# Moving the last batch's transposes to SyncE's queue, with a new instruction order, in a kernel for gated linear attention followed by a mixer

## The chip, the cores and the metric

One Trainium2 chip, one of its cores. The metric is device time in microseconds (us). A run more than 1.5% above the fastest of its kernel counts as slow and is left out of the ratios (the medians given are of all runs). The kernel before took 174.36 us (median of 3 runs, 174.34 to 175.11); its profiled execution took 174.75 us, of which the profile's span covers 173.0 us.

## The reference

```python
state = alpha[:, :, t, :, None] * state + einsum('bhd,bhe->bhde', k[:, :, t], v[:, :, t])   # for t in 768 steps
y[:, :, t] = einsum('bhd,bhde->bhe', q[:, :, t], state)
# x = y with heads side by side: (4 batches, 768, 384)
h = x.transpose(0, 2, 1) @ U @ V              # low rank (32), along the sequence
u = x + h.transpose(0, 2, 1)
out = u + maximum(u @ w_ch1, 0) @ w_ch2       # 384 -> 1536 -> 384
```

Four batches, 8 heads of 48, 768 steps. The kernel works in chunks of 128 steps, six to a batch.

## The kernel before

The program does not fix the order of its instructions by hand. Each step is added to a plan with a cost for each engine that may run it, a priority, what it reads and what it writes. A list scheduler then picks, at each moment of its own model of time, the step that can start first, and emits the instructions in that order. Semaphores are added afterwards, so a wrong cost in the plan gives no wrong result; it gives a wait on the chip.

```python
if eng == "SP":                                  # a DMA issued by SyncE
    dma = max(dma, t + 600.0) + cost
    clock[eng] = max(t + 450.0, dma - 3500.0)
    end = dma + 2000.0
...
if eng == "PE" and "PE" in u.engs:
    u.est = max(u.est, end)
else:
    u.est = max(u.est, done + u.slack)           # slack: 150 ns for batches 1 to 3
```

For one chunk of the recurrence (q and k are scaled by the decays, transposed, multiplied into scores):

```python
P.add({"PE": mm(*[C] * 4)}, lambda e: f_tr(rk, tk), r=[rk], w=[tk], ...)      # 4 transposes into PSUM
P.add({"PE": mm(*[C] * 4)}, lambda e: f_tr(rq, tq), r=[rq], w=[tq], ...)
P.add({"DVE": 335, "ACT": 500}, lambda e: f_ev(e, kT, tk), r=[tk], w=[kT], ...)  # eviction to SBUF
P.add({"DVE": 335, "ACT": 500}, lambda e: f_ev(e, qT, tq), r=[tq], w=[qT], ...)
...
P.add({"PE": mm(*[C] * 4)}, f_sc, r=[kT, qT], w=[sc[0], sc[1]], mode="R", ...)   # the score block
```

The mixer of a batch: `utx` is the low-rank sum over all chunks of x; each chunk gets a low-rank matmul and the addition that makes u; u is transposed on TensorE into uT; 72 matmuls of 384 columns (u with w_ch1) and 72 more (with w_ch2) follow. The multiplications of one batch are scheduled among the recurrence of the next, and `LEAD` says how far behind the recurrence their priority is:

```python
LEAD = 3.0
def mlp_prio(b, x):
    return ((b + 1) * NC + LEAD + x * NC) * 100.0
```

## Time and profile before

| | before |
|---|---|
| median time | 174.36 us |
| span of the profile | 173.0 us |
| first matmul of a multiplication (with w_ch1, first batch) | 30.69 us |
| end of the last matmul | 169.49 us |
| the stretch between these two | 138.80 us |
| TensorE idle within it | 2.86 us |

The prediction shows most of what matters. These three stretches add where the idle time lies. In such a line come the stretch, its length, and busy us (with the number of instructions) of PE, PEld (weight loads), DVE, ACT and POOL, then the granted clock, the DMA share and GB/s. Length less PE busy is idle: 2.23, 0.63 and 0 us.

```profile
31.00:60.00 29.00, 26.77 (x373) 16.97 (x374) 24.44 (x54) 21.73 (x57) 13.08 (x21) 1.00 1.03 259
60.00:100.00 40.00, 39.37 (x490) 26.72 (x488) 28.24 (x55) 27.73 (x68) 18.76 (x25) 1.00 1.11 203
100.00:140.00 40.00, 40.00 (x414) 25.89 (x413) 26.75 (x50) 21.82 (x52) 10.91 (x13) 1.00 0.36 85
```

### The profile page before, as it was taken

The page shows a single profiled execution, that of the slowest core. Times are in us where ns is not written, and L with a number is a line of the kernel's source. Part 1 is how long each engine was busy: PE and PEld are TensorE (multiplying, and loading weights), DVE is VectorE, ACT ScalarE, POOL GpSimd, SP SyncE. Part 2 cuts the span into 40 slices and gives each one's busy share as a digit, 9 for nine tenths or more (in the row PEclk, how much of TensorE's full clock was granted, in tenths as well). Part 3 has the DMA queues.
Part 4 walks back from the last instruction along what each step waited for, and adds up shares of the span by engine and source line. Part 5 has one row for each costly group of instructions (what it writes and reads, how often), then busy time and mean ns, then how long its engine had stood idle before and what let it go on. Part 6 is the DMA issues. An engine that isn't in the chain of part 4 may idle for free.

```text
span 173.0 us, 4823 instructions
## 1 busy us (share of the span) xinstructions
PE 161.9 (94%) x1862; PEld 104.2 (60%) x1862; DVE 109.0 (63%) x232; ACT 104.1 (60%) x247; POOL 59.5 (34%) x97
## 2 busy tenths in 40 slices
PE   7688998899996999999998999999999999999991
PEld 2355765566564776676676657666666566656560
DVE  4589685598996986958675559976474294000231
ACT  4588773779785767558949436638783210996000
POOL 8056366247331765255155414910430000000000
PEclk9999699999999999999999999999999999999998
DMA  5999989999998999999989999611000212100222
GB/s 140 266 249 260 267 255 335 258 300 330 269 267 200 178 207 211 214 222 221 230 147 206 189 166 258 170 58 37 0 0 4 91 45 91 51 0 0 91 93 91
DMA packets 83031, 28.82 MB, mean 167 GB/s; under 512 B 76832, under 2 KB 82976, under 8 KB 83008
## 3 DMA queue, kind: packets, MB, share of 16 engines
q1 hardware_dynamic: 83008, 28.52, 72.0%
q8 instruction: 14, 0.23, 0.6%
q14 instruction: 9, 0.07, 0.2%
HBM read 23.79 MB, written 4.72 MB: 165 GB/s over the span
## 4 chain that ended last, share of the span: by engine, by line
PE 60%; DMA 19%; SPq 15%; issue 2%; POOL 1%; ACT 1%; DVE 0%; ACTq 0%; POOLq 0%
PE ps L772 27%; PE ps L749 16%; SPq L342 10%; DMA io<-in_v_dram 8%; DMA io<-in_moe_w_ch_dram 5%; SPq L317 3%; DMA io<-in_alpha_dram 3%; PE ps L584 3%; DMA io<-in_k_dram 3%; PE ps L605 2%; PE ps L712 2%; PE ps L722 2%; PE ps L664 1%; PE ps L554 1%; PE ps L418 1%
## 5 line engine op out<-in xcount | busy, mean ns | idle before, releaser
L749 PE MATMUL ps<-uT,w_sb 128*128 128x384 bf16 x288 | 53.1, 326 | 0.0
L772 PE MATMUL ps<-w_sb,h1t 128*128 128x384 bf16 x288 | 52.8, 326 | 0.0
L759 ACT ACTIVATE h1t<-ps 128x384 bf16<-128x384 f32 x73 | 35.2, 494 | 8.8 <-PE ps L749 8.5
L772 PEld LDWEIGHTS <-h1t 128*128 128x128 bf16 x288 | 26.1, 98 | 16.0 <-issue 1.0
L749 PEld LDWEIGHTS <-w_sb 128*128 128x128 bf16 x288 | 26.1, 98 | 15.4
L779 DVE TENSOR_TENSOR ou<-ub,ps 128x384 f32<-128x384 bf16 x24 | 13.2, 551 | 27.6 <-PE ps L772 27.3
L302 POOL CAST rv<-io 128x384 bf16<-128x384 f32 x19 | 11.2, 590 | 35.7 <-DMA io<-in_v_dram 30.7
L615 DVE TENSOR_TENSOR pm<-ps,maskc 128x512 bf16<-128x512 f32 x24 | 15.7, 685 | 6.7 <-PE ps L605 6.5
L572 POOL TENSOR_TENSOR rk<-io,ai 128x384 bf16<-128x384 f32 x12 | 11.0, 916 | 20.2 <-ACT ai L565 18.7
L761 DVE TENSOR_SCALAR h1t<-ps 128x384 bf16<-128x384 f32 x23 | 12.6, 552 | 7.4 <-PE ps L749 4.8
L456 DVE TENSOR_TENSOR pm<-ps,maskp 128x512 bf16<-128x512 f32 x24 | 15.8, 681 | 0.7 <-ACT h1t L759 0.5
L298 ACT CAST xb<-ps 128x192 bf16<-128x192 f32 (+1 forms) x23 | 8.8, 392 | 11.6 <-PE ps L664 7.6
L298 ACT COPY kt<-ps 128x512 bf16<-128x512 bf16 x17 | 10.0, 586 | 5.8 <-PE ps L584 5.3
L713 DVE TENSOR_TENSOR ub<-xb,ps 128x384 bf16<-128x384 bf16 x24 | 12.1, 547 | 1.2 <-PE ps L712 1.2
L298 ACT COPY qt<-ps 128x512 bf16<-128x512 bf16 x17 | 11.3, 663 | 1.6 <-PE ps L418 1.0
L302 POOL CAST w_sb<-io 128x384 bf16<-128x384 f32 x21 | 10.8, 527 | 3.8 <-DMA io<-in_moe_w_ch_dram 3.5
L572 POOL TENSOR_TENSOR rq<-io,aa 128x384 bf16<-128x384 f32 x12 | 11.6, 967 | 0.0
L375 ACT ACTIVATE lt<-io 128x384 bf16<-128x384 f32 x12 | 6.4, 530 | 5.2 <-DMA io<-in_alpha_dram 5.2
L298 ACT COPY uT<-ps 128x768 bf16<-128x768 bf16 x4 | 3.2, 799 | 8.6 <-PE ps L722 5.1
L547 ACT ACTIVATE lt<-io 128x384 bf16<-128x384 f32 x12 | 6.5, 542 | 2.0 <-DMA io<-in_alpha_dram 2.0
L398 ACT ACTIVATE ai<-ps 128x384 bf16<-128x384 f32 x12 | 5.9, 493 | 2.8 <-PE ps L391 2.8
L565 ACT ACTIVATE ai<-ps 128x384 bf16<-128x384 f32 x12 | 6.0, 500 | 2.4 <-PE ps L557 2.0
(114 smaller groups left out, 249.3 us busy)
## 6 DMA issues: line engine op xcount, KB each, us to landing
io<-in_alpha_dram SPq DMA_DIRECT2D x24, 192.0 KB, 4.3
io<-in_k_dram SPq DMA_DIRECT2D x24, 192.0 KB, 4.5
io<-in_q_dram SPq DMA_DIRECT2D x24, 192.0 KB, 4.3
io<-in_v_dram SPq DMA_DIRECT2D x24, 192.0 KB, 4.5
io<-in_moe_w_ch_dram SPq DMA_DIRECT2D x24, 192.0 KB, 4.4
out_dram<-ou SPq DMA_DIRECT2D x24, 192.0 KB, 1.9
u_in<-in_moe_U_dram SPq DMA_DIRECT2D x1, 96.0 KB, 4.6
v_in<-in_moe_V_dram SPq DMA_DIRECT2D x1, 96.0 KB, 4.3
```

The lines of the kernel that those rows point to most:

```text
L298: nc.scalar.copy(dst, src)
L302: nc.gpsimd.tensor_copy(dst, src)
L342: lambda e: nc.sync.dma_start(t().rearrange("p (h j) d -> p h (j d)", j=2), src[b, hs, sl, :].rearrange("h (p j) d -> p h (j d)", j=2)),
L456: nc.vector.tensor_tensor(dst, s2, maskp.to_broadcast([C, 2, 2, C]), op=ALU.mult)
L572: eng.tensor_tensor(dst()[:, :, 0:D], a(), x(), op=ALU.mult)
L615: nc.vector.tensor_tensor(pm()[:, :, par, :], s2, maskc.to_broadcast([C, HP, C]), op=ALU.mult)
L713: P.add({"DVE": 465}, lambda e, c=c, hb=hb: nc.vector.tensor_tensor(ub()[:, c, :], xb()[:, c, :], hb()[:, 0:DM], op=ALU.add), r=[hb] + xk( ...
L749: nc.tensor.matmul(hb()[:, 0:TW], lhsT=w1_sb[:, ct, jt * 128 : (jt + 1) * 128], rhs=uT()[:, ct, tt * TW : (tt + 1) * TW], start=(ct == 0), ...
L759: nc.scalar.activation(dst, hb()[:, 0:TW], AF.Relu)
L761: nc.vector.tensor_scalar_max(dst, hb()[:, 0:TW], 0.0)
L772: nc.tensor.matmul(hb()[:, 0:DM], lhsT=h1()[:, jt, c * C : (c + 1) * C], rhs=w2_sb[:, jt, :], start=(jt == 0), stop=(jt == NJ - 1),)
L779: P.add({"DVE": 468}, lambda e: nc.vector.tensor_tensor(ou(), ub()[:, c, :], hb()[:, 0:DM], op=ALU.add), r=[hb, (ub, c)], w=[ou], prio=-100)
```

## The change

Its intent: take transposes off TensorE in the last batch, as the loads run out, by letting DMAs issued by SyncE transpose from SBUF to SBUF (through what is called the crossbar here); make the plan's order sturdier (slack, a bonus for staying in the matmul mode, buffers taken to be free 200 ns later) and its cost for loads higher; and add the first batch's low-rank sums within the output's PSUM group instead of in VectorE.

```diff
+    EASE = 200.0
+    STAY = 20.0                         # TensorE: prefer the mode it is in
+    TRD = {(3, c) for c in range(2, NC)}   # q, k of these chunks by crossbar
+    SL = 300.0                          # slack, 150 before
+    TRU = (3,)                          # u of this batch by crossbar
+            if eng == "SP" and op.mode == "X":
+                dma = max(dma, t) + cost
+                clock[eng] = t + cost
+                end = dma + 850.0
-                b.last = max(b.last, done)
+                b.last = max(b.last, done + self.EASE)
-    LEAD = 3.0
+    LEAD = 5.0
-                    {"SP": 750.0},      # a load of the first two batches
+                    {"SP": 790.0},
-            P.add({"SP": 1000.0}, ...   # a load of the last two
+            P.add({"SP": 1080.0}, ...
-        P.add({"SP": 540.0}, ...        # a weight
+        P.add({"SP": 590.0}, ...
# ... u_in and v_in: prio 2.5 -> 4.5
+        if (b, c) in TRD:
+            for ring, dst in ((rk, kT), (rq, qT)):
+                P.add({"SP": 1250.0},
+                    lambda e, ring=ring, dst=dst: nc.sync.dma_start(dst(), ring().rearrange("t h w -> t (h w)"), transpose=True),
+                    r=[ring], w=[dst], prio=-0.5, mode="X")
+        else:                           # as before, on TensorE
# ... stage_mix
+            if b in TRU:
+                P.add({"SP": 1250.0},
+                    lambda e, c=c: nc.sync.dma_start(uT()[:, :, c * C : (c + 1) * C], ub()[:, c, :], transpose=True),
+                    r=[(ub, c)], w=[(uT, c)], prio=-0.5, mode="X")
# ... mlp2, first batch: the low-rank matmul is the last of the output's group,
#     and the output is x + group instead of u + group
+                if low:
+                    nc.tensor.matmul(hb()[:, 0:DM], lhsT=vm_sb[:, c * C : (c + 1) * C], rhs=utx(), start=False, stop=True)
```

More of the change, by code (lines that the diff above doesn't have):

```diff
@@ L120, in run @@
                 t0 = min(t for t, _ in ok)
-                t1, op = min(((t, o) for t, o in ok if t <= t0 + 1.0), key=lambda x: (x[1].prio, x[1].i))
+                t1, op = min(((t, o) for t, o in ok if t <= t0 + 1.0), key=lambda x: (x[1].prio + (self.STAY if eng == "PE" and x[1].mode != mode else 0.0), x[1].i))
                 key = (t1, t1 + op.engs[eng])
@@ L136, in run @@
             cost = op.engs[eng]
-            if eng == "SP":
+            if eng == "SP" and op.mode == "X":
+                dma = max(dma, t) + cost
+                clock[eng] = t + cost
+                end = dma + 850.0
+            elif eng == "SP":
                 dma = max(dma, t + 600.0) + cost
@@ L304, in small @@
     def small():
-        P.add({"SP": 450.0}, lambda e: nc.sync.dma_start(u_in, moe_U.rearrange("(c p) r -> p c r", p=128)), w=["u_in"], prio=2.5)
-        P.add({"SP": 500.0}, lambda e: nc.sync.dma_start(v_in, moe_V), w=["v_in"], prio=2.5)
+        P.add({"SP": 450.0}, lambda e: nc.sync.dma_start(u_in, moe_U.rearrange("(c p) r -> p c r", p=128)), w=["u_in"], prio=4.5)
+        P.add({"SP": 500.0}, lambda e: nc.sync.dma_start(v_in, moe_V), w=["v_in"], prio=4.5)
         P.add({"POOL": 300}, lambda e: nc.gpsimd.tensor_copy(u_sb, u_in), r=["u_in"], w=["u"], prio=395)
@@ L316, in weight @@
         t = Buf(io)
-        P.add({"SP": 540.0}, lambda e: nc.sync.dma_start(flat(t), src), w=[t], prio=prio)
+        P.add({"SP": 590.0}, lambda e: nc.sync.dma_start(flat(t), src), w=[t], prio=prio)
         P.add(engs, lambda e: copy(e, dst, flat(t)), r=[t], w=[key], prio=pr)
@@ L348, in load @@
             sl = slice(c * C, (c + 1) * C)
-            P.add({"SP": 1000.0}, lambda e: nc.sync.dma_start(t(), src[b, :, sl, :].rearrange("h t d -> t h d")), w=[t], prio=key)
+            P.add({"SP": 1080.0}, lambda e: nc.sync.dma_start(t(), src[b, :, sl, :].rearrange("h t d -> t h d")), w=[t], prio=key)
         for c in range(NC):
@@ L364, in stage_pair @@
         pr = (b * NC + u) * 100.0
-        sl = 0.0 if b == 0 else 150.0
+        sl = 0.0 if b == 0 else SL
         at, qt, kt, vt = tiles[b, u]
@@ L543, in stage_gla @@
         pr = kk * 100.0
-        sl = 150.0
+        sl = SL
         at, qt, kt, vt = tiles[b, c]
@@ L576, in stage_gla @@
         P.add(both, lambda e: f_scale(e, rq, qt, aa), r=[qt, aa], w=[rq], prio=pr + 11, slack=sl)
-        tk, tq = Buf(bank), Buf(bank)
         kT, qT = Buf(kts), Buf(qts)
-        def f_tr(ring, tb):
-            t = bf(tb()).rearrange("p (e c) -> p e c", c=C)
-            for p in range(HP):
-                nc.tensor.matmul(
-                    t[:, p, :],
-                    lhsT=ring()[:, 2 * p : 2 * p + 2, :].rearrange("t h w -> t (h w)"),
-                    rhs=ident, start=True, stop=True, is_transpose=True,
-                )
@@ L590, in f_ev, with f_tr @@
-        def f_ev(e, dst, tb):
-            copy(e, dst(), bf(tb()).rearrange("p (e c) -> p e c", c=C)[:, 0:HP, :])
-        P.add({"PE": mm(*[C] * 4)}, lambda e: f_tr(rk, tk), r=[rk], w=[tk], prio=pr + 18, slack=sl)
-        P.add({"PE": mm(*[C] * 4)}, lambda e: f_tr(rq, tq), r=[rq], w=[tq], prio=pr + 18, slack=sl)
-        P.add({"DVE": 335, "ACT": 500}, lambda e: f_ev(e, kT, tk), r=[tk], w=[kT], prio=pr + 8, slack=sl)
-        P.add({"DVE": 335, "ACT": 500}, lambda e: f_ev(e, qT, tq), r=[tq], w=[qT], prio=pr + 8, slack=sl)
+        if (b, c) in TRD:
+            for ring, dst in ((rk, kT), (rq, qT)):
+                P.add(
+                    {"SP": 1250.0},
+                    lambda e, ring=ring, dst=dst: nc.sync.dma_start(dst(), ring().rearrange("t h w -> t (h w)"), transpose=True),
+                    r=[ring], w=[dst], prio=-0.5, mode="X",
+                )
+        else:
+            tk, tq = Buf(bank), Buf(bank)
+            def f_tr(ring, tb):
+                t = bf(tb()).rearrange("p (e c) -> p e c", c=C)
+                for p in range(HP):
+                    nc.tensor.matmul(
+                        t[:, p, :],
+                        lhsT=ring()[:, 2 * p : 2 * p + 2, :].rearrange("t h w -> t (h w)"),
+                        rhs=ident, start=True, stop=True, is_transpose=True,
+                    )
+            def f_ev(e, dst, tb):
+                copy(e, dst(), bf(tb()).rearrange("p (e c) -> p e c", c=C)[:, 0:HP, :])
+            P.add({"PE": mm(*[C] * 4)}, lambda e: f_tr(rk, tk), r=[rk], w=[tk], prio=pr + 18, slack=sl)
+            P.add({"PE": mm(*[C] * 4)}, lambda e: f_tr(rq, tq), r=[rq], w=[tq], prio=pr + 18, slack=sl)
+            P.add({"DVE": 335, "ACT": 500}, lambda e: f_ev(e, kT, tk), r=[tk], w=[kT], prio=pr + 8, slack=sl)
+            P.add({"DVE": 335, "ACT": 500}, lambda e: f_ev(e, qT, tq), r=[tq], w=[qT], prio=pr + 8, slack=sl)
@@ L674, in stage_mix @@
         pr = (b * NC + NC - 0.5) * 100.0
-        sl = 0.0 if b == 0 else 150.0
+        sl = 0.0 if b == 0 else SL
         xu = Buf(bank)
@@ L708, in stage_mix @@
                     P.add({"ACT": 390, "DVE": 470}, lambda e, j=j, tt=tt, tb=tb: copy(e, uT()[:, j, tt * TW : (tt + 1) * TW], tb[j]()[:, 0:TW]), r=[tb[j]], w=[(uT, tt, j)], prio=pr + tt, slack=sl)
-            pr = mlp_prio(0, 0.3)
+            return utx
         for c in range(NC):
-            hb = Buf(bank, 3 if b == 0 else 0)
+            hb = Buf(bank, 2)
             P.add({"PE": mm(DM)}, lambda e, c=c, hb=hb: nc.tensor.matmul(hb()[:, 0:DM], lhsT=vm_sb[:, c * C : (c + 1) * C], rhs=utx(), start=True, stop=True), r=[utx, ("vm", c // NT)], w=[hb], prio=pr + c, slack=sl)
             P.add({"DVE": 465}, lambda e, c=c, hb=hb: nc.vector.tensor_tensor(ub()[:, c, :], xb()[:, c, :], hb()[:, 0:DM], op=ALU.add), r=[hb] + xk(b, xb, c), w=[(ub, c)], prio=pr + c, slack=sl)
-            if c % 2 == 1 and b > 0:
+            if b in TRU:
+                P.add(
+                    {"SP": 1250.0},
+                    lambda e, c=c: nc.sync.dma_start(uT()[:, :, c * C : (c + 1) * C], ub()[:, c, :], transpose=True),
+                    r=[(ub, c)], w=[(uT, c)], prio=-0.5, mode="X",
+                )
+            elif c % 2 == 1:
                 ub2 = Buf(bank)
@@ L732, in stage_mix @@
                 P.add({"DVE": 450, "ACT": 710}, f_ev, r=[ub2], w=[(uT, c // 2)], prio=pr + c, slack=sl)
+        return utx
     def mlp_prio(b, x):
@@ L743, in mlp1 @@
                 need = [(uT, tt, j) for j in range(NCT)]
+            elif b in TRU:
+                need = [(uT, c) for c in range(tt * NT, (tt + 1) * NT)]
             else:
@@ L763, in mlp1, with mlp2 @@
             P.add({"ACT": 395, "DVE": 470}, g, r=[hb], w=[(h1, tt, jt)], prio=-100)
-    def mlp2(b, ub, h1, c):
+    def mlp2(b, xb, ub, utx, h1, c):
         hb = Buf(bank, RES[b])
@@ L768, in mlp2, with f @@
         for g in range(3):
-            def f(e, g=g):
+            low = b == 0 and g == 2
+            def f(e, g=g, low=low):
                 for jt in range(4 * g, 4 * g + 4):
@@ L773, in f @@
                         hb()[:, 0:DM], lhsT=h1()[:, jt, c * C : (c + 1) * C], rhs=w2_sb[:, jt, :],
-                        start=(jt == 0), stop=(jt == NJ - 1),
+                        start=(jt == 0), stop=(jt == NJ - 1 and not low),
                     )
-            P.add({"PE": mm(*[DM] * 4)}, f, r=[(h1, tt, jt) for jt in range(4 * g, 4 * g + 4)] + [("w2", jt) for jt in range(4 * g, 4 * g + 4)], w=[hb], prio=mlp_prio(b, 0.5 + c / 12.0 + g / 36.0))
+                if low:
+                    nc.tensor.matmul(hb()[:, 0:DM], lhsT=vm_sb[:, c * C : (c + 1) * C], rhs=utx(), start=False, stop=True)
+            P.add({"PE": mm(*[DM] * (5 if low else 4))}, f, r=[(h1, tt, jt) for jt in range(4 * g, 4 * g + 4)] + [("w2", jt) for jt in range(4 * g, 4 * g + 4)] + ([utx] if low else []), w=[hb], prio=mlp_prio(b, 0.5 + c / 12.0 + g / 36.0))
         ou = Buf(outs)
-        P.add({"DVE": 468}, lambda e: nc.vector.tensor_tensor(ou(), ub()[:, c, :], hb()[:, 0:DM], op=ALU.add), r=[hb, (ub, c)], w=[ou], prio=-100)
+        P.add({"DVE": 468}, lambda e: nc.vector.tensor_tensor(ou(), (xb if b == 0 else ub)()[:, c, :], hb()[:, 0:DM], op=ALU.add), r=[hb] + (xk(b, xb, c) if b == 0 else [(ub, c)]), w=[ou], prio=-100)
         P.add({"SP": 550.0}, lambda e: nc.sync.dma_start(out[b, c * C : (c + 1) * C, :], ou()), r=[ou], prio=-1)
@@ L794 @@
                 st[0] = stage_gla(b, c, st[0], xb)
-        stage_mix(b, xb, ub, uT)
+        utx = stage_mix(b, xb, ub, uT)
         mlp1(b, uT, h1, 0)
@@ L798 @@
         for c in range(NC):
-            mlp2(b, ub, h1, c)
+            mlp2(b, xb, ub, utx, h1, c)
     P.run()
```

## The prediction

> **What bounds the kernel now.** I read the page's busy shares first, then the chain that ended last, then stretches of 2 to 20 us, then TensorE's waits and its instructions in order of time.
>
> ```profile
> span 173.0 us, 4823 instructions
> ...
> PE 161.9 (94%) x1862; PEld 104.2 (60%) x1862; DVE 109.0 (63%) x232; ACT 104.1 (60%) x247; POOL 59.5 (34%) x97
> ...
> DMA  5999989999998999999989999611000212100222
> ```
>
> TensorE is the busiest engine by far; VectorE and ScalarE have a third of the span free. The DMA row, 40 slices of 4.3 us, says that loads fill the queues for about 26 slices (to 112 us) and that they are nearly empty afterwards. So a transfer that is added after 112 us finds free engines.
>
> The 2 us stretches show where TensorE really is full (columns: stretch, its length, then busy us of PE, PEld, DVE, ACT, POOL with counts, the granted clock, DMA share, GB/s):
>
> ```profile
> 18.00:20.00 2.00, 2.00 (x47) 1.45 (x45) 1.11 (x4) 1.64 (x6) 0.88 (x2) 0.53 1.14 255
> ...
> 52.00:54.00 2.00, 0.55 (x21) 0.39 (x19) 1.31 (x4) 0.19 (x1) 0.50 (x1) 1.00 0.92 207
> ...
> 90.00:92.00 2.00, 1.37 (x20) 0.95 (x19) 0.58 (x2) 1.59 (x4) 0.35 (x1) 1.00 0.95 188
> ...
> 140.00:142.00 2.00, 2.00 (x18) 1.31 (x16) 2.00 (x6) 0.43 (x1) 0.00 (x0) 1.00 0.14 50
> ```
>
> Idle time of TensorE is 173.0 - 161.9 = 11.1 us. From 54.0 us to the last matmul at 169.5 us it has one hole only (0.63 us before 91.5 us); everything there is packed, and taking work away takes time away. The rest is 1.2 us before the first matmul, 3.5 us after the last (result addition, store, end), and 5.8 us before 54 us. Of TensorE's waits (us in total, times, longest) these matter:
>
> ```profile
> PE ps L479 <- POOL rv L302: 1.7, 2, 1.5
> PE ps L418 <- DVE rk L405: 1.0, 3, 0.5
> PE ps L384 <- ACT lt L375: 0.7, 1, 0.7
> PE ps L605 <- ACT qt L298: 0.6, 1, 0.6
> ```
>
> The 1.5 is the hole at 52.5 us: a v tile arrived late (in the chain, its load takes 6.04 us from 47.36 us, then GpSimd casts it). The 0.7 is at 32.6 us, the first decay tile of the second batch. The 0.6 is the hole at 91 us. The last pieces of the chain show the end game, which is matmul and nothing else:
>
> ```profile
> 143.16 0.34 PE ps L722 x6
> 143.50 2.60 PE ps L772 x16
> 146.10 11.70 PE ps L749 x72
> 157.80 11.71 PE ps L772 x72
> 169.54 0.55 DVE ou L779
> ```
>
> 72 matmuls of 384 columns take 11.70 us, so one costs 0.1625 us; six 128-column transposes take 0.34 us, so one costs about 0.056 us.
>
> **What the Trainium skill says.** The skill's front page, "Trainium Kernel Development and Optimization", section "Performance Expectations", calls matmul busy time a bad metric of the distance to peak. I use it only to find holes, and take costs from start-to-start times in the chain. "TensorE: Matmul & The Clock Gate", section "Part 4: PE-mode transpose", gives about 390 ns for an isolated 128x128 transpose and notes that it ends in PSUM, so an eviction follows. The trace agrees on the eviction (the kt copies are 0.586 us each on ScalarE) but not on the price: 216 to 219 ns is the record of one, and 0.056 us is what one takes in a row, so that is what its removal is worth. "VectorE: DVE Perf Modes", section "The three transpose paths", gives 1309 ns for a 128x128 transpose in the DMA crossbar, landing in SBUF; nothing in the trace of before shows one. "DMA: Bandwidth & Descriptors", section "Rules for kernel authors", says that two transposes of different queues must be serialized and that one next to ordinary DMAs needs nothing; here all fourteen come from SyncE's queue.
>
> **The change part by part.**
>
> 1. Transposes leave TensorE. The last batch's q and k of four chunks: 2 x 4 x 4 = 32 matmuls; its u: 6 x 3 = 18 matmuls. 50 x 0.056 = 2.8 us. All lie between 103 and 144 us, where TensorE had no hole, so all of it should come off the end. With them go 8 evictions of 512 columns and 3 of 768 from ScalarE and VectorE (about 8 x 0.6 + 3 x 0.8 = 7 us), which hide behind TensorE anyway.
>
> 2. Fourteen crossbar transposes come in on SyncE's queue: eight of 128x512 and six of 128x384. The order of the compiled queue shows what surrounds them. The last pair for q and k stands behind the store of the second batch's last chunk. After that store's matmuls TensorE's order still has 45 matmuls of 384 columns and about 1.5 us of small ones before the scores of chunk 4, and 12 more and another score block before those of chunk 5: 45 x 0.1625 + 1.5 = 8.8 us and 8.8 + 2.0 + 0.3 = 11.1 us. The queue must in that time issue the store and three transposes (chunk 4's q; chunk 5's k and q). At 1.3 us each (my estimate, from the skill's figure for 128x128; a tile four times as large may cost more) and some 2 us for landing, as the stores take, chunk 4 is there after about 1.2 + 1.3 + 2 = 4.5 us and chunk 5 after 7.1 us. So each transpose could cost twice the estimate (2.6 us: 5.8 and 11.0 us) before a wait appears. For u, the third transpose stands behind the store of the third batch's second chunk, and 49 matmuls, 8.0 us, run between that and the first use, against some 4.5 us needed; the last stands behind the fourth chunk's store and also has about 4 us to spare. I book no wait: 0 us.
>
> 3. The first batch's low-rank sums are accumulated into the output's PSUM group. The six 384-column matmuls are only moved, but six VectorE additions of 0.547 us (3.3 us) disappear, and six PSUM banks are no longer taken in the crowded stretch from 43 to 58 us. TensorE: 0 us; VectorE was not the bound.
>
> 4. The new order. Fillers rise from 14 to 17, in places where TensorE waits anyway: 0 to +0.3 us. The u_in and v_in loads move behind eight others, so chunk tiles of the first batch arrive up to about 1.7 us earlier, but the batch's last loads do not, and the first 31 us end with them: about 0. At the second batch's start 12 instead of 6 matmuls of the first multiplication stand before the first decay sum: 6 x 0.1625 = 1.0 us, more than the wait of 0.74 us. Before the block that waited 1.46 us there are now 20 instead of 4 matmuls of the second multiplication and four low-rank ones fewer, 12 x 0.1625 = 1.95 us of work more, which exceeds the wait. Against this, that work then lacks later: where 91.5 us had the hole, 15 fewer matmuls have been passed than before. So I credit 2.2 us gained up to 54 us, 0.6 us lost again in new holes between 54 and 100 us, and 0.3 us for fillers and the unforeseen: net 1.3 us.
>
> Sum: 2.8 + 1.3 = 4.1 us. 174.36 - 4.1 = 170.3 us, a gain of 2.3%.
>
> **The rivals.**
> - The transposes are slow or the queue stalls behind a store. A queue in order makes chunk 4 and 5 wait for stores of another batch. For it: in the profile the output stores wait 56.7 us in total on that queue. Against: the margins above. If a 128x512 transpose held the queue for 4 us, chunk 5 would be some 5 us late, the time about 174 to 176 us.
> - Loads take over as the bound: DMA is full to 112 us, and running ahead of it by 4 us just moves the wait. For it: the hole at 91 us is a load's. Against: the last batch's tiles were all there by 112 us and used until 135 us, so a lag there is swallowed by matmuls of the third batch. If the order's gain is lost this way, only the transposes' 2.8 us stay: 171.5 us.
> - The order removes nearly all holes between 31 and 100 us (2.8 us with the one at 91): 174.36 - 5.6 = 168.8 us.
>
> **Range and chances.** Two per cent is 170.9 us; the middle lies only 0.6 us below it. The transposes' share is firm, the order's share is uncertain by about 1.5 us either way, and a slow transpose is a small tail. Range 168.7 to 172.0 us. Faster by over 2%: 0.62; within: 0.35; slower: 0.03.
>
> **What would show it.** TensorE's busy time should fall from 161.9 us by 2 to 3 us, with 32 transposes of q and k fewer (64 left of 96) and 18 of u (36 left of 54). There should be no wait of scores on a transposed tile in the last batch, and none of the last 144 matmuls on uT; the last 144 should still take 23.4 us. The holes at 32 and 52 us should be gone. The prediction is wrong if score blocks or the last multiplication wait for SyncE's queue, if the time before 31 us grows, or if holes between 54 and 100 us sum to over 2 us.

## The result, and the profile after

The changed kernel took 169.94 us (median of 4 runs, 169.19 to 170.98) against 174.6 us for the kernel before in the same session: ratio 0.9734, with a 95% interval of 0.9675 to 0.9793. A ratio here is the mean time of one kernel's fast runs over that of the other's in the same rounds, so it is not quite the ratio of the medians. In a later session, on another set of rounds, the unedited changed kernel had 0.9754 (0.9713 to 0.9794).

The page of the changed kernel, the same rows as the prediction shows of before:

```profile
span 168.0 us, 4727 instructions
...
PE 157.3 (94%) x1810; PEld 100.4 (60%) x1815; DVE 106.7 (64%) x225; ACT 101.0 (60%) x242; POOL 53.6 (32%) x92
...
DMA  5999999999999989999999999998510254200222
```

TensorE's share is the same 94%, of a span that is 5.0 us shorter. 1815 weight loads against 1862 are 47 fewer: 50 transposes less, three fillers more. (Five matmul records are missing here, so the busy time of 157.3 us is a little low; a second profile has 159.1 us.) The DMA row is fuller at slices 26 to 30, where q's and k's crossbar transposes now stand among loads that come later than before (the last is issued at 114.24 us, before at 106.50 us), and at slices 33 to 35, where u's are.

The same three stretches: idle is now 0.34, 0 and 0.12 us.

```profile
31.00:60.00 29.00, 28.66 (x390) 18.34 (x389) 24.99 (x53) 21.89 (x57) 10.49 (x18) 1.00 1.02 260
60.00:100.00 40.00, 40.00 (x527) 26.85 (x526) 32.94 (x64) 31.09 (x77) 20.57 (x27) 1.00 1.09 203
100.00:140.00 40.00, 39.88 (x354) 24.52 (x349) 22.35 (x41) 16.72 (x40) 7.67 (x10) 1.00 0.66 129
```

The end of TensorE's timeline (start, length, line, shapes, count), which answers to the end of the chain before. 48 matmuls with w_ch2 cover the crossbar's work on u, and the last 144 take as long as before, 11.86 us for each 72 by this view's records, with no wait:

```profile
132.86 7.96 PE L801 MATMUL ps<-w_sb,h1t 128*128 128x384 bf16 x48
140.66 11.86 PE L776 MATMUL ps<-uT,w_sb 128*128 128x384 bf16 x72
152.36 11.86 PE L801 MATMUL ps<-w_sb,h1t 128*128 128x384 bf16 x72
```

Where the 5.0 us of the span went. The multiplications start at 30.78 us (30.69 before), so the first stage is the same. From there to the end of the last matmul (164.22 us) is 133.44 us against 138.80: 5.36 us less. Of this, 2.86 - 0.46 = 2.40 us are idle time of TensorE, and the remaining 2.96 us are work, of which the transposes are 2.8 us by the prediction's estimate. The tail after the last matmul is 0.27 us longer (168.0 - 164.22 against 173.0 - 169.49), and 0.09 us are lost at the start: 5.36 - 0.36 = 5.0 us.

### The profile page after: what moved, and what is told of

Its sections match the earlier page's. It is cut to its first block, busy times and chain, and to the rows that moved or that the text cites. A ratio compares the mean times of both kernels' runs of the same rounds, so it can differ in the third digit from the quotient of the medians.

```text
span 168.0 us, 4727 instructions
## 1 busy us (share of the span) xinstructions
PE 157.3 (94%) x1810; PEld 100.4 (60%) x1815; DVE 106.7 (64%) x225; ACT 101.0 (60%) x242; POOL 53.6 (32%) x92
## 4 chain that ended last, share of the span: by engine, by line
PE 78%; SPq 14%; DMA 4%; issue 1%; DVE 0%; ACT 0%; ACTq 0%
PE ps L801 29%; PE ps L776 27%; SPq L351 9%; SPq L326 4%; DMA io<-in_alpha_dram 4%; PE ps L622 2%; PE ps L601 2%; PE ps L427 2%; PE ps L729 2%; PE ps L681 1%; PE ps L563 1%; PE ps L745 1%; PE ps L454 1%; PE ps L679 1%; PE ps L540 1%
## 5 line engine op out<-in xcount | busy, mean ns | idle before, releaser
L810 DVE TENSOR_TENSOR ou<-ub,ps 128x384 f32<-128x384 bf16 x18 | 10.0, 553 | 31.2 <-PE ps L801 31.2
L311 POOL CAST rv<-io 128x384 bf16<-128x384 f32 x17 | 8.6, 504 | 24.8 <-DMA io<-in_v_dram 22.5
L307 ACT COPY kt<-ps 128x512 bf16<-128x512 bf16 x14 | 8.2, 587 | 7.4 <-PE ps L601 5.1
L581 POOL TENSOR_TENSOR rq<-io,aa 128x384 bf16<-128x384 f32 x12 | 11.3, 940 | 0.2 <-ACT tot L576 0.2
L311 POOL CAST w_sb<-io 128x384 bf16<-128x384 f32 x19 | 9.6, 521 | 4.0 <-DMA io<-in_moe_w_ch_dram 3.8
L414 POOL TENSOR_TENSOR rq<-io,aa 128x384 bf16<-128x384 f32 x6 | 5.9, 980 | 11.7 <-ACT tot L409 10.5
L414 DVE TENSOR_TENSOR rk<-io,ai 128x384 bf16<-128x384 f32 x12 | 7.9, 658 | 2.7 <-ACT ai L407 2.5
L730 DVE TENSOR_TENSOR ub<-xb,ps 128x384 bf16<-128x384 bf16 x18 | 8.9, 548 | 0.3 <-PE ps L729 0.3
L574 ACT ACTIVATE ai<-ps 128x384 bf16<-128x384 f32 x12 | 6.0, 498 | 4.5 <-PE ps L566 4.5
L384 ACT ACTIVATE lt<-io 128x384 bf16<-128x384 f32 x12 | 6.4, 535 | 2.9 <-DMA io<-in_alpha_dram 2.9
L309 DVE CAST xb<-ps 128x192 bf16<-128x192 f32 (+1 forms) x15 | 6.1, 405 | 1.9 <-PE ps L540 1.4
```

Of the source, the lines that this page charges most:

```text
L307: nc.scalar.copy(dst, src)
L311: nc.gpsimd.tensor_copy(dst, src)
L414: eng.tensor_tensor(jh(dst()[:, :, 0:D]), raw(a), jh(x()), op=ALU.mult)
L581: eng.tensor_tensor(dst()[:, :, 0:D], a(), x(), op=ALU.mult)
L810: P.add({"DVE": 468}, lambda e: nc.vector.tensor_tensor(ou(), (xb if b == 0 else ub)()[:, c, :], hb()[:, 0:DM], op=ALU.add), r=[hb] + (xk( ...
```

## The experiments

Twelve kernels ran. Each was correct. All ratios are to the kernel before; its median was 175.71 us (chip 14), 175.47 us (chip 7). By the 2% rule most of the single parts below count as "same" or "unclear"; the argument rests on whether an interval excludes 1.

### Adding and taking the two halves: order_only and transposes_only

The changed kernel with every transpose back on TensorE:

```diff
-    TRD = {(3, c) for c in range(2, NC)}
+    TRD = set()
-    TRU = (3,)
+    TRU = ()
```

> The changed kernel with all transposes back on TensorE; the new order rules and the spread low-rank sums stay. Theory (two separate gains: 2.8 us of transposes taken off a packed TensorE, and about 2 us of holes closed by the new order): about 172.5 us, ratio to before 0.988 (0.983 to 0.993), TensorE without the holes at 32 and 52 us. Rival A (the order gives it all, the transposes were hidden): about 170 us, ratio 0.974. Rival B (the order gives nothing by itself, it only makes room for the crossbar): about 174.4 us, ratio 1.00.

The kernel before with the crossbar transposes and nothing else:

```diff
# changed kernel with: EASE 0, STAY 0, SL 150, LEAD 3, load costs 540, 750 and 1000,
# u_in and v_in at prio 2.5, low-rank sums of the first batch as before
```

> The kernel before with only the fourteen crossbar transposes in place of the 50 matmuls and 11 evictions; order rules, queue times and low-rank sums as before. Theory: about 171.8 us, ratio 0.984 (0.979 to 0.990), with the holes near 52 and 91 us still there. Rival A: about 174.4 us, ratio 1.00, because the saved matmuls come back as waits. Rival B: about 174 us or more, with waits of scores or of the last multiplication for the queue of SyncE, as the plan has no measured queue times.

Measured: order_only 173.87 us, ratio 0.9892 (0.984 to 0.9944), as the theory of two separate gains had it. transposes_only 176.06 us, ratio 1.0003 (0.9946 to 1.0061): that theory expected 0.984 here and falls. The 50 matmuls were gone and nothing was won. The timeline of TensorE in that run shows what ate it:

```profile
141.34 3.41 PE L801 MATMUL ps<-w_sb,h1t 128*128 128x384 bf16 x20
146.91 13.52 PE L776 MATMUL ps<-uT,w_sb 128*128 128x384 bf16 x72 [2.15 <-DMA uT<-ub]
```

In brackets stands the idle time before the group and what ended it. Only 20 matmuls, some 3.3 us, cover the crossbar's work on u; then TensorE waits 2.15 us for uT. And the 72 matmuls that follow take 13.52 us instead of 11.86. The stretches show why (the column after POOL is the granted clock):

```profile
146.00:148.00 2.00, 1.09 (x4) 0.58 (x5) 0.00 (x0) 0.00 (x0) 0.00 (x0) 0.72 0.59 160
148.00:150.00 2.00, 2.00 (x8) 0.88 (x6) 0.00 (x0) 1.00 (x3) 0.00 (x0) 0.50 0.28 54
150.00:152.00 2.00, 2.00 (x13) 1.15 (x12) 0.00 (x0) 1.76 (x4) 0.00 (x0) 0.93 0.27 53
```

After the wait the clock is down to half for a while, which costs 13.52 - 11.86 = 1.66 us more. Wait and clock together, 3.8 us, exceed the 2.8 us that the transposes save. The old order also kept its other holes (1.33, 0.72, 0.55 and 0.96 us between 33 and 93 us). This profile is of the slowest of the six runs (177.20 us), so its parts add up to more than the 1.0003 of the ratio.

### Is TensorE really full where the transposes were? extra_pe50

The changed kernel, in exactly its order, with 50 useless transposes put back:

```diff
 def f_sc(e):
+    if (b, c) in TRD:
+        for ring in (rk, rq):          # 4 transposes each into sc[0], overwritten by the scores
+            ...
 # and before each low-rank matmul of the last batch, into the same bank:
+    for j in range(NCT):
+        nc.tensor.matmul(t[:, j, :], lhsT=xb()[:, c, j * C : (j + 1) * C], rhs=ident, ..., is_transpose=True)
```

> The changed kernel in its very order, with 50 redundant 128x128 transposes added to TensorE (8 before each of the last batch's four score blocks that read crossbar tiles, 3 before each of its six low-rank matmuls), written into the PSUM bank that the next matmul overwrites, with no eviction. The crossbar transposes stay. Theory: 50 x 0.056 = 2.8 us longer than the changed kernel, about 172.7 us, ratio to before 0.989. Rival A (TensorE has slack there): about 170 us, ratio 0.974. A third view, that it was the evictions on ScalarE and VectorE that cost, also gives about 170 us.

Measured: 173.21 us, ratio 0.9841 (0.9782 to 0.99), against 0.9734 and 0.9754 for the changed kernel: 0.9 to 1.1% longer, that is 1.5 to 1.9 us, less than the 2.8 us expected, though the intervals reach 2.8 us. The profile lets one take the idle time out: from the first multiplication to the last matmul 136.63 us, of which 0.84 us idle, so 135.79 us of work, against 133.44 - 0.46 = 132.98 us in the changed kernel. The difference is 2.81 us, and 50 x 0.056 is 2.8 us; against the second profile of the changed kernel (after_again, below) it is 135.79 - 133.18 = 2.61 us. The transposes on TensorE cost about what the chain of the kernel before said, and it is the matmuls, not the evictions: this run adds no eviction.

### How much room has SyncE's queue? dma_twice

```diff
+    nc.sync.dma_start(scr(), <same source>, transpose=True)     # before each of the fourteen; 3 scratch tiles in turn
     nc.sync.dma_start(dst(), <source>, transpose=True)
```

> The changed kernel with each of the fourteen crossbar transposes preceded by one of the same source into a scratch tile: 28 in all on SyncE's queue, each about 1.2 to 1.3 us of issue. My prediction said that each could cost twice the estimate before a wait appears, so theory: same as the changed kernel, about 170 us, ratio 0.974 (0.968 to 0.980), the score blocks of chunks 4 and 5 at most just beginning to wait. Rival (the queue is already near its limit, and its order behind the stores makes it the next bound): 2 to 8 us longer, 172 to 178 us, with TensorE idle before the last scores or before the last batch's first multiplication.

Measured: 186.74 us, ratio 1.0596 (1.0537 to 1.0655). The rival is right, and by more than it said. TensorE's waits in this run (us in total, times, longest) name the queue twice:

```profile
PE ps L632 <- DMA qt<-rq: 7.5, 4, 3.2
PE ps L789 <- DMA uT<-ub: 3.7, 2, 2.9
```

All four score blocks wait. That is 11.2 us; and in the stretches 114 to 118 and 131 to 135 us the granted clock is 0.57, which costs 2 x 4 x 0.43 = 3.4 us more. Together 14.6 us, against 184.7 - 169.8 = 14.9 us between this profile and the second one of the changed kernel. Not every wait brings the clock down: after the longest one for uT it stays at 1.00 (160 to 168 us), and 36 matmuls take 6.01 us, the full speed.

```profile
163.13 6.01 PE L789 MATMUL ps<-uT,w_sb 128*128 128x384 bf16 x36 [2.91 <-DMA uT<-ub]
```

The margin that I had worked out, some 4 us, is not there for q and k. The queue of SyncE in the changed kernel, in order of time (start, length of the issue, what):

```profile
112.35 0.53 SPq L811 DMA_DIRECT2D out_dram<-ou  x1
112.97 1.22 SPq L592 DMA_TRANSPOSE qt<-rq  x1
114.24 0.58 SPq L358 DMA_DIRECT2D io<-in_v_dram  x1
114.91 0.53 SPq L811 DMA_DIRECT2D out_dram<-ou  x1
115.54 1.22 SPq L592 DMA_TRANSPOSE kt<-rk  x1
116.86 0.53 SPq L811 DMA_DIRECT2D out_dram<-ou  x1
117.48 2.32 SPq L592 DMA_TRANSPOSE qt<-rq  x1
119.91 1.21 SPq L592 DMA_TRANSPOSE kt<-rk  x1
121.21 1.23 SPq L592 DMA_TRANSPOSE qt<-rq  x1
```

From 103.5 to 122.4 us, 17 issues (eight transposes, five stores, four loads) follow each other with hardly a gap (0.45 us at most); the queue itself is full. The store at 116.86 us could have gone at about 113.9 us, 1.2 us after the second batch's last matmul ended at 112.7 us, and then chunk 4's q behind it, which GpSimd had made by 112.50 us. Chunk 5's k and q could not: GpSimd makes them by 116.56 and 117.43 us, and the queue sends them at 119.91 and 121.21 us. The last q transpose is issued at 121.21 us and lands 2.4 us later, at 123.6 us. The score block that reads it:

```profile
123.93 0.40 PE L622 MATMUL ps<-qt,kt 48*128 48x128 bf16 x8
```

The margin is 0.3 us. For chunk 4 it is 0.3 us too (117.48 + 3.7 = 121.2 against 121.54 us), for chunk 3 1.4 us. For chunk 2 there is none: q lands at 105.31 + 3.8 = 109.1 us, the block begins at 109.27 us, and TensorE had been idle for 0.12 us before it. That is the 0.12 us of the third stretch above. Chunk 2's transposes stand among the last loads; the prediction worked out chunks 4 and 5 only. For u the margins are as predicted: the third transpose lands at 137.6 us against a first use at 140.66 us.

### The changed kernel again, and u's part of the loss: after_again and tr_qk_old

> The changed kernel itself, unedited, so that it stands on the same chip and in the same rounds as the next three: ratio to before 0.973 (0.967 to 0.979), as first measured.

Measured: 171.18 us, ratio 0.9754 (0.9713 to 0.9794). Its profile shows the same score block, chunk 2's, waiting longer:

```profile
111.16 0.40 PE L622 MATMUL ps<-qt,kt 48*128 48x128 bf16 x8 [1.20 <-DMA qt<-rq]
```

In this run q's transpose landed 4.0 us after its issue at 107.0 us, with loads still in flight. extra_pe50, which has the same order, waits there too:

```profile
110.93 0.40 PE L627 MATMUL ps<-qt,kt 48*128 48x128 bf16 x8 [0.62 <-DMA qt<-rq]
```

So in all three profiles of this order the block waits for SyncE's queue: 0.12, 1.20 and 0.62 us.

tr_qk_old is transposes_only with u left on TensorE:

```diff
-    TRU = (3,)
+    TRU = ()
```

> The kernel before with crossbar transposes for q and k of the last batch's four chunks only (32 matmuls); u stays on TensorE, order rules as before. Theory (in the run of all fourteen under the old order, u's crossbar ate the gain: TensorE waited 2.1 us for the last batch's uT and then ran 4 us at a reduced clock): without u's the wait and the clock drop vanish, ratio 0.990 (0.984 to 0.996), no wait for uT. Rival (the q and k transposes under the old order gain nothing either): ratio 1.00.

Measured: 173.61 us, ratio 0.9893 (0.9855 to 0.9931), no wait for uT and a granted clock of 1.0. So under the old order q's and k's crossbar gains about its 32 x 0.056 = 1.8 us (1.1% of 175.5 us is 1.9 us), and u's threw it away.

### What makes room for u: tr_lead and trd_b3all

```diff
# tr_lead: transposes_only with
-    LEAD = 3.0
+    LEAD = 5.0
```

> All fourteen crossbar transposes in the kernel before, with one order rule changed: LEAD 5 in place of 3, which puts the multiplications later against the recurrence. By the compiled order, 75 matmuls of 384 columns (12.2 us) now stand between the last batch's low-rank matmuls and the first use of its uT, against 20 (3.3 us) where all fourteen ran under the old order, and 56 (9.1 us) in the changed kernel. Theory (this cover decides whether u's crossbar transposes cost anything): no wait for uT, no clock drop, ratio 0.980 (0.974 to 0.987). Rival (the slack terms and the queue times are what makes room): the gain stays away, ratio 0.995 to 1.00.

Measured: 174.09 us, ratio 0.9889 (0.9828 to 0.9949). There is no wait for uT and no clock drop, so the cover does decide. But the gain is smaller than expected; the holes between 31 and 140 us sum to 4.74 us, against 3.95 us in transposes_only and 2.86 us before (1.22, 0.88, 0.73 and 1.45 us at 32.5, 46.4, 96.1 and 100.4 us). Both sides were half right.

```diff
# trd_b3all: the changed kernel with
-    TRD = {(3, c) for c in range(2, NC)}
+    TRD = {(3, c) for c in range(0, NC)}
```

> The changed kernel with q and k of all six chunks of the last batch in the crossbar, four transposes more (16 matmuls less, 0.9 us). By the compiled order only 4 matmuls of 384 columns (0.65 us) stand after the last low-rank one, and 12 after the first five, before the first use of uT. Theory: TensorE waits about 3 us for uT and then runs at a reduced clock for some 4 us; 2 to 5 us longer than the changed kernel, ratio 0.985 to 1.00. Rival (fewer matmuls on a packed TensorE always shorten): ratio 0.968.

Measured: 174.57 us, ratio 0.9871 (0.9805 to 0.9938), although 16 matmuls fewer stand on TensorE. Three of its six runs count as slow, as one (171.69 us) lies well below the rest, and the profile is of one of those three (175.19 us); so I read the wait alone from it. The wait that the compiled order had announced is there, followed by slow matmuls (13.54 us for 72):

```profile
144.58 13.54 PE L776 MATMUL ps<-uT,w_sb 128*128 128x384 bf16 x72 [3.14 <-DMA uT<-ub]
```

So what covers u's six crossbar transposes decides, and it can be counted in the compiled order: 20 matmuls of 384 columns were too few (a 2.15 us wait), 12 too few (3.14 us), 56 and 75 enough.

### The parts of the order: queue_times_only, slack_only, lowrank_back

queue_times_only is order_only with EASE 0, STAY 0, SL 150, LEAD 3 and the low-rank sums as before; slack_only is order_only with the old load costs and priorities (540, 750, 1000; 2.5) and the low-rank sums as before.

```diff
# the two halves of the order rules
-    {"SP": 540.0} {"SP": 750.0} {"SP": 1000.0}, prio=2.5      -> queue_times_only
+    {"SP": 590.0} {"SP": 790.0} {"SP": 1080.0}, prio=4.5
-    EASE 0, STAY 0, SL 150, LEAD 3                            -> slack_only
+    EASE 200, STAY 20, SL 300, LEAD 5
```

> The kernel before with the measured queue times of the loads and the later load of the two small tensors only; slack terms and LEAD as before, no crossbar. If the queue times close the holes: ratio 0.990 (0.985 to 0.995). If the slack does: 0.998 to 1.003. If neither alone does and both are needed: both runs at 0.995 to 1.00.

> The kernel before with the slack terms, the mode bonus and LEAD 5, but the old queue times of the loads; no crossbar, low-rank sums as before. If the slack is what closes the holes at 32, 52 and 91 us: ratio 0.989 (0.984 to 0.994) like the whole order. If the measured queue times do it: ratio 0.998 to 1.005, with holes of 1 us and more between 30 and 100 us. I lean to the second, as LEAD 5 under the old queue times had three holes of 0.7 to 1.5 us.

Measured: queue_times_only 171.99 us, ratio 0.9809 (0.9776 to 0.9843); slack_only 178.84 us, ratio 1.0181 (1.0131 to 1.0231). The stretches of the first (two lines) and of the second (two lines):

```profile
31.00:60.00 29.00, 28.21 (x402) 18.77 (x400) 24.85 (x55) 22.57 (x57) 13.07 (x23) 1.00 1.00 258
60.00:100.00 40.00, 40.00 (x488) 26.85 (x484) 30.02 (x58) 27.26 (x65) 17.68 (x25) 1.00 1.09 201
```

```profile
31.00:60.00 29.00, 26.32 (x354) 17.23 (x354) 23.52 (x52) 21.68 (x56) 11.91 (x20) 1.00 1.00 256
60.00:100.00 40.00, 37.47 (x506) 25.21 (x501) 30.55 (x60) 26.03 (x67) 17.49 (x25) 1.00 1.05 195
```

With the new load costs and priorities alone, TensorE has 0.79 us of idle time between 31 and 100 us; with the slack alone, 2.68 + 2.53 = 5.21 us. (The second profile fell in a slow run; its fast runs, 177.19 to 179.69 us, are slow enough by themselves.) Telling the plan that loads take 5 to 9% longer, together with the later load of the two small tensors (prio 4.5), closed the holes; the two were not tried apart. Slack and LEAD, on a plan that still believes loads to be faster, opened new ones. That the new costs are nearer to the chip's own times is not shown here: no run compares them with a load alone.

```diff
# lowrank_back: the changed kernel with the first batch's low-rank sums as before
-            return utx          # (in the first batch, no u is made)
+            pr = mlp_prio(0, 0.3)
...
-            low = b == 0 and g == 2
+            low = False
```

> The changed kernel with the first batch's low-rank sums as before (own PSUM group, six VectorE additions of 0.55 us); transposes and order rules of the change stay. Theory (this part only moves six matmuls and unloads VectorE, which is not the bound): ratio 0.975 (0.969 to 0.981), as the changed kernel. Rival (it is what closed the holes near 52 us, by freeing PSUM banks): ratio 0.983 or more, with holes between 43 and 60 us.

Measured: 169.47 us, ratio 0.9654 (0.9608 to 0.9701). Moving the sums back costs nothing; this run is even lower than the changed kernel on the same chip (0.9754, 0.9713 to 0.9794). The two were not in the same rounds, so the 1% between them is not settled. One difference is visible: here the replanned order left chunk 2's scores 1.2 us of margin (q landed at 105.5 + 3.3 = 108.8 us, the block began at 110.03 us), and no score block waited.

### A version with a truer landing time: imp_land

```diff
-                end = dma + 850.0
+                end = dma + 2200.0
```

> The changed kernel with one number of its plan changed: a crossbar transpose is taken to land 2.2 us after its issue instead of 0.85 us (measured: 2.3 to 5.0 us from the start of a 1.2 us issue). By the compiled order, 12 more matmuls of 384 columns and a decay sum stand before the scores of chunk 2 of the last batch, which waited 1.2 us for its crossbar tile in one profile of the changed kernel and 0.1 us in another. Theory (those scores are on the edge): no wait for a crossbar tile, 0 to 1.2 us shorter than the changed kernel, ratio 0.971 (0.965 to 0.976). Rival (the wait is paid back by TensorE elsewhere): as the changed kernel, 0.974, with a wait somewhere else.

Measured: 170.23 us, ratio 0.9668 (0.9618 to 0.9719), in the same rounds as lowrank_back, and no wait for a crossbar tile (margin of chunk 2: 1.5 us). Its profile fell in a slow run, so I use it for order and waits only: after the first multiplication TensorE has no idle time in it at all down to 140 us. Both this and lowrank_back have lower ratios than the changed kernel; which of the two is better, these runs do not tell, and against the changed kernel they were not run side by side. That the longer landing time is what helped is so not shown.

### All runs together

Taken from the profiles: the first multiplication, the end of the last matmul, idle time of TensorE between them (31 to 140 us, and the wait for uT where there was one), and what is left. "Left" is TensorE's work under that order, at the clock that it was granted. The profiles of trd_b3all, slack_only and imp_land are of slow runs and stand apart, as does dma_twice.

| kernel | ratio | first | last ends | stretch | idle | left |
|---|---|---|---|---|---|---|
| before | 1 | 30.69 | 169.49 | 138.80 | 2.86 | 135.94 |
| changed | 0.9734 | 30.78 | 164.22 | 133.44 | 0.46 | 132.98 |
| after_again | 0.9754 | 31.13 | 166.12 | 134.99 | 1.81 | 133.18 |
| extra_pe50 | 0.9841 | 31.60 | 168.23 | 136.63 | 0.84 | 135.79 |
| order_only | 0.9892 | 29.92 | 168.31 | 138.39 | 1.94 | 136.45 |
| queue_times_only | 0.9809 | 31.02 | 167.10 | 136.08 | 0.89 | 135.19 |
| transposes_only | 1.0003 | 30.60 | 172.12 | 141.52 | 6.10 | 135.42 |
| tr_qk_old | 0.9893 | 30.38 | 168.30 | 137.92 | 3.15 | 134.77 |
| tr_lead | 0.9889 | 30.15 | 168.97 | 138.82 | 4.74 | 134.08 |
| lowrank_back | 0.9654 | 30.36 | 164.05 | 133.69 | 0.61 | 133.08 |

Two things can be read here. "Left" falls into groups by the transposes: 135 to 136.5 us where all are on TensorE, 134.8 with 32 fewer, 133 to 134.1 with 50 fewer (transposes_only too, once the 1.66 us of reduced clock are taken out). And "first" varies by over 1 us from profile to profile, by 0.8 us (30.78, 31.13, 31.60) among the three of the changed kernel's order, so differences of half a per cent between single times should not be explained.

## Why the prediction was right, and where it was not

The time, 170.3 us, came out at 169.94 us: 4.7 us less than before in the same session, where 4.1 us were forecast. In part that was luck: the waits for the queue, booked as 0 us, and the order's gain, booked too low, have opposite signs.

**Step 1, transposes leave TensorE: right.** 2.8 us predicted; 2.96 us less work in the profile, and 2.6 to 2.8 us when fifty were put back without moving anything else.

**Step 2, fourteen transposes on the queue cost nothing: the entry of 0 us was nearly right, its working was right for u and wrong for q and k.** The prediction says that "each transpose could cost twice the estimate (2.6 us: 5.8 and 11.0 us) before a wait appears". dma_twice doubled them and cost 15 us. By the prediction's own sign ("wrong if score blocks or the last multiplication wait for SyncE's queue") this step failed. What failed is the count of what the queue has to issue: I took the store and the three transposes behind it as starting with the store's matmuls, with an empty queue in front. In the trace the queue was busy with hardly a pause from 103.5 us, the store went out 3 us later than that, chunk 5's k and q were not even made before 116.56 and 117.43 us, and the margins of q and k were 1.4 us or less. Chunk 2, for which I worked out none, waited: 0.12 us in one profile of the changed kernel, 1.2 us in the other. That it was not more was luck and not reasoning. The unit cost, which I had feared most, was the better part: 1.19 to 1.33 us for most issues, against the 1.3 us that I took.

**Step 3, low-rank sums: right that they give TensorE nothing.** lowrank_back has a lower ratio without them. That they help by freeing PSUM banks finds no support.

**Step 4, the order: right in sign, off in size and in place.** Credited: 2.2 us up to 54 us, 0.6 us lost between 54 and 100 us, 0.3 us for fillers: net 1.3 us. Measured: 2.23 - 0.34 = 1.9 us gained between 31 and 60 us, and 0.63 us gained, not lost, between 60 and 100 us; 0.12 us lost after; the start and the tail took 0.36 us. Net 2.0 us. The mis-sized term is the 0.6 us of new holes: the hole at 91 us went away. In the second profile 2.23 us are gained up to 60 us and only 0.02 us between 60 and 100 us, as new holes stand at 73 and 88 us (0.19 and 0.42 us); neither profile shows a loss there. The order by itself, in order_only, gained 1.1% (0.6 to 1.6%), 1.9 us.

**What the prediction did not see** is that the two halves need each other. It added 2.8 us and 1.3 us. Under the old order the transposes gained nothing (1.0003), as 20 matmuls could not cover u's transposes; LEAD 5 provides the cover, as tr_lead shows. And within the order the gain comes from the longer load times with the later small loads (0.9809 alone), while slack with LEAD 5 alone loses 1.8%. Why slack_only lost so much was not taken apart further. Nor was order_only with the old low-rank sums run, so its 0.8% above queue_times_only may be the slack, LEAD or the sums.

Of the rivals, the first ("the queue stalls behind a store") is what lies just beyond this version, and what happens in dma_twice; the second, that loads take the gain, did not come: idle time between 60 and 100 us did not rise (0.63 us before, 0 and 0.61 us in the two profiles). The third, nearly all holes between 31 and 100 us gone, came closest in the profile: 5.36 us less between first and last multiplication, where it said 5.6 us. Its time, 168.8 us, was not reached.

## What to carry to other kernels

Before work is moved from a full engine to a queue that issues in order, add up all that the queue issues in that stretch, not only what stands right behind the wait that you look at; and count, in the compiled order, how much work covers the new latency. In this list-scheduled kernel the costs of the loads, with two small loads moved, changed the idle time more than all safety terms, so try the costs before adding slack. A hole of 2 us on TensorE can cost nearly twice its length, through the clock (2.15 + 1.66 us in transposes_only), but does not always.

## What the Trainium skill lacked or had wrong

- "VectorE: DVE Perf Modes", section "The three transpose paths", gives 1309 ns for a crossbar transpose of 128x128. That section has no figure for larger tiles or for issue and landing apart. Here the issue took 1.19 to 1.33 us in most cases for 128x384 and 128x512 alike (up to 2.32 us), and in the changed kernel's profile the landing came 2.3 to 2.8 us after the start of the issue for ten of the fourteen, 3.1 to 5.0 us for the other four, three of them issued before 112 us, among loads.
- "DMA: Bandwidth & Descriptors", section "Rules for kernel authors", says that a transpose next to ordinary DMAs needs nothing. For correctness the runs agree. That rule says nothing of time: the longest landings (5.0 and 3.8 us, issued at 103.53 and 105.31 us) came among loads, the 2.3 us of u's when only stores were left, but no run tests the neighbours alone. The queue's issue time, 17 issues in 18.9 us, was the limit here.
- "TensorE: Matmul & The Clock Gate", section "Why this matters for your kernels", warns of gaps of more than about 3 us between bursts. Here a wait of 2.15 us, and nothing longer, was followed by a granted clock of 0.72, 0.50 and 0.93 in the next three stretches of 2 us, 1.66 us lost; a wait of 1.20 us was not. The length alone does not decide: in dma_twice a wait of 2.91 us was followed by a clock of 1.00.
- "TensorE: Matmul & The Clock Gate", section "Part 4: PE-mode transpose", gives 275 to 390 ns as the duration of a transpose; that section does not say what one takes within a full stream. Here its removal was worth some 0.056 us, as fifty put back showed (2.61 and 2.81 us against the two profiles of the changed kernel).
